# Lightning attention and top-1 routing on one core: half of an early first layer in Strassen's form, and the loads and lists around it

## The chip, the cores and the metric

The kernel runs on one NeuronCore of a Trainium2 chip. The metric is the device time of one execution in microseconds (us). PE (TensorE) does the matmuls, DVE (VectorE), ACT (ScalarE) and POOL (GpSimd) the elementwise work; SP (SyncE) only issues DMAs here. POOL also issues the indirect DMAs that gather rows by a list of indices, scatter rows, and store places into lists; ACT issues the stores of attention rows.

## The reference

Causal attention with a decay per head (4 batches, 8 heads, 768 positions, head width 64, all float32), then a top-1 mixture of experts over the 3072 rows of 512 that it gives:

```python
intra = einsum(qb, kb) * Dmask @ vb            # per block of 64, plus a carried state
inter = (qb * lam_pow) @ kv_state
x = attn_out.transpose(0, 2, 1, 3).reshape(3072, 512)
expert = argmax(x @ w_gate); gate = softmax(x @ w_gate)[expert]
for e in range(8):
    h  = maximum(x[mask_e] @ w1[e], 0)         # 512 -> 1024
    out[mask_e] = gate * (h @ w2[e])           # 1024 -> 512
```

## The kernel before, in words

**Attention.** The kernel goes through 12 steps: six chunks of 128 positions, each for two pairs of batches. A step transposes q and k, forms scores, applies the decay on DVE, and writes its finished rows to `xs` in DRAM. The gate's logits of each step are turned into a place on the chosen expert's list; POOL stores those places into `slots` in DRAM (L467), some of them behind a memset of `between` that fixes their position in POOL's stream.

**Passes.** A pass is a list of tokens of one expert: gathered rows `xg`, their transpose `xgT`, the first layer `hT` (8 chunks `fc` of 128 hidden features, contracted over 4 chunks `dc` of 128), the second layer, and a scatter of the rows. Expert 5's first 256 places are a pass of their own, 0a, which starts while the last attention step is still running. Pass 0b holds the rest of expert 5 (128 places). Passes 1 to 7 are the other experts, fullest first, with up to 418 places. 0a and 0b share one pair of weight tiles.

**Strassen's form.** Where a product of 2x2 blocks can be made with 7 block products in place of 8, the kernel does so (Winograd's variant): four sums of the left side, s1 to s4, four of the right side, t1 to t4, and sums u2, u3, u4 of the products. Before the change that holds for 0a's second layer (`form_early`, sums of `w2t` in `second_sums` and of `hT` in `left_of`, all on DVE), for the one tile of 0b's second layer (`lone_tile`, two products at a time on half of PE's rows each), and for both layers of passes 1 to 7 (`hidden_fast`, `outputs_across`). The first layers of 0a and 0b (`hidden`, L606) are plain products.

**What sets the order.** Each engine runs one stream of instructions in order. The framework writes that order when the kernel is built, with a planner that may move instructions; `pin` (keep_in_program_order) fixes those it is given among each other. DMAs of SP go out in the order of SP's stream. In program order, around the change: the last attention steps; `gather_early` (L1135 on), which issues the two gathers of 0a and then, when they have landed, the load of `w2t` (L1141); `turn(passes[0])`; the last stores of places; the counting that orders the experts (L1219 to L1254); the read of 0b's list, the value load that tells SP which expert is second, the read of pass 1's list (L496), the load of pass 1's `w1t` as one DMA of 2 MB (L202), and the gathers of 0b (one) and of pass 1 (four) (L527); then the loop over the passes. For pass 0a the loop makes `second_sums` on DVE (L683), `hidden`, `split(passes[2])` (copies of pass 1's rows into 16-bit planes on ACT, L575, and eight DMA transposes on SP, L577), SP's reads of the later lists, and `outputs_early`, which calls `turn(passes[1])` (0b's transposes on PE, L592) before its last product. For pass 0b it makes `hidden`, `first_sums` of pass 1's `w1t` on POOL (s3 and s1 at once, s2 and s4 in `finish`, L652 and L655), the gathers of pass 2, the sums of `later_sums`, `join` (two copies on ACT that put pass 1's `xgT` together, L585), `token_sums` on DVE (L713), and `lone_tile` (L782 and the sums after it, L818 to L835). `finish` waits for `token_sums`. The tile `xgT` has one buffer for all passes.

`form_early` ends with:

```python
        give(0, 1, product(a.s4, b.b22), u4)
        ahead()
        give(1, 0, product(a.a22, b.t4), u3)
```

Of the kernel before, what the change touches and what calls it, by code (L numbers as in the profile page):

```python
# [22 lines left out]
def kernel(  # L23
# [562 lines left out]

    def turn(m, pin=lambda inst: inst):
        m.xgT = ffn.tile([P, DC, m.n], F32, tag="xgT", name="xgT", bufs=1)
        for c in range(0, DC, 2):
            tp = bank(next(tp_banks), [P, 2, m.n], "tp")  # L590
            for dc, (t, w) in itertools.product(range(c, c + 2), enumerate(m.widths)):
                pin(nc.tensor.transpose(tp[:, dc - c, t * P:t * P + w],  # L592
                                        m.xg[t // 2][:w, t % 2, dc * P:(dc + 1) * P],
                                        ident[:w, :w]))

            if c == 0:
                nc.vector.tensor_copy(m.xgT[:, c:c + 2, :], tp)
            else:
                nc.scalar.copy(m.xgT[:, c:c + 2, :], tp)
# [12 lines left out]
    DH, FH = DC // 2, F // 2  # L612

    def form(product, sums_of, temps, give, first=nothing):

# [10 lines left out]
        give(0, 1, product(a.s4, b.b22), u2)  # L626
        give(1, 0, product(a.a22, b.t4), u3)

    def form_early(product, sums_of, temps, give, ahead):

        a, b = sums_of
        p1, u2, u3, u4 = temps
        nc.vector.tensor_copy(p1, product(a.a11, b.b11))
        give(0, 0, product(a.a12, b.b21), p1)
        nc.vector.tensor_add(u2, product(a.s2, b.t2), p1)
        nc.vector.tensor_add(u3, product(a.s3, b.t3), u2)
        p5 = product(a.s1, b.t1)
        give(1, 1, p5, u3)
        nc.vector.tensor_add(u4, p5, u2)
        give(0, 1, product(a.s4, b.b22), u4)  # L640
        ahead()
        give(1, 0, product(a.a22, b.t4), u3)
# [39 lines left out]
    def vector_sub(o, x, y):  # L682
        pin(nc.vector.tensor_sub(o, x, y))  # L683
# [107 lines left out]

    def outputs_early(m, w2, ahead):
        a = left_of(m.hT, 0, P, pair_rooms_of_sums())
        for make in (a.s3_made, a.s1_made, a.s2_made, a.s4_made):
            make()
        o, outs, temps = pair_rooms()

# [5 lines left out]

        form_early(block, (a, w2), temps, give, ahead)
        for i in range(2):
            scatter(at(m, i)[1], o[i])

# [327 lines left out]
    def gather_early(other):  # L1135
# [119 lines left out]


    def next_pass(i):
        e = nc.values_load(turns[0:1, i:i + 1], min_val=0, max_val=E - 1,
                           engines=[mybir.EngineType.SP])
        passes.append(make_pass(e, 0, CAPS[i], str(i)))  # L1260

    passes.append(make_pass(FIRST, EARLY, CAPS[0] - EARLY, "0b"))
    next_pass(1)
    later = []
    weights.append(load_weights(passes[2].w, later))
    for m in passes[1:]:
        fetch(m)
    last = E
    for i in range(last + 1):
# [16 lines left out]
        if i == 0:  # L1286
            w2 = second_sums(w2t, vector_sub)
        if i < 2:
            hidden(m, w1t)
# [78 lines left out]
```

## Time and profile before

| | us |
|---|---|
| median of 3 runs | 433.4 (432.65 to 434.5) |
| the profiled execution | 435.07 |
| its span, first to last instruction | 432.8 |
| PE busy | 421.3 (97%) |
| DVE, POOL, ACT busy | 266.0, 257.5, 176.8 |

The span is 2.3 us shorter than the profiled execution's time; that rest lies around the first and the last instruction. The profile gives for each instruction its start, its duration, and what ended its engine's idle time before it. A float32 matmul stands in the records as two (pass 0a's 32 matmuls of the first layer are 64 records). Records of pipelined matmuls overlap, so the pace of PE is read from the distance of their starts and not from the duration of one. The granted TensorE clock over the run is 0.997 of full speed, which is the level of 2.4 GHz nearly throughout.

### The profile page before, as it was taken

The numbers are of one execution on the slowest core, as the hardware profiler recorded it, in microseconds if no ns is written. First come the engines' busy times: TensorE is split into PE (matmuls) and PEld (weight loads), VectorE is DVE, ScalarE is ACT, GpSimd is POOL, SyncE is SP. The second block draws the span as 40 slices with busy tenths as digits, with TensorE's granted clock in tenths as the row PEclk, the third lists the DMA queues.
The fourth block names the chain that finished last, engine by engine and source line by source line (L and its number), as shares of the span: only waits on it lengthen the run. The fifth ranks groups of instructions, "written<-read, shape, count | busy, mean of one in ns | idle before, by whom it ended". The sixth has DMA issues, their size and how long they took to land.

```text
span 432.8 us, 9573 instructions
## 1 busy us (share of the span) xinstructions
PE 421.3 (97%) x3699; PEld 393.9 (91%) x3699; DVE 266.0 (61%) x585; ACT 176.8 (41%) x319; POOL 257.5 (59%) x205
## 2 busy tenths in 40 slices
PE   8999999999999999999999999999999999999993
PEld 6888898888888897999999999999999999999972
DVE  6656656566766647686547757755575664775463
ACT  3366545555542423450554155245424605422221
POOL 5243457373344368777948757693885887749032
PEclk9999999999999999999999999999999999999998
DMA  9999989999985758976369857965975894753122
GB/s 174 211 245 229 220 213 213 233 193 249 292 283 149 265 105 234 325 246 237 52 139 190 332 76 157 319 179 112 299 246 81 196 384 80 153 186 56 20 83 63
DMA packets 164727, 83.49 MB, mean 193 GB/s; under 512 B 146019, under 2 KB 146063, under 8 KB 164672
## 3 DMA queue, kind: packets, MB, share of 16 engines
q1 hardware_dynamic: 155024, 63.21, 61.2%
q0 software_dynamic: 5712, 13.26, 10.2%
q10 hardware_dynamic: 3936, 6.31, 4.2%
q8 instruction: 31, 0.51, 0.5%
q14 instruction: 24, 0.20, 0.2%
HBM read 58.96 MB, written 13.09 MB: 166 GB/s over the span
## 4 chain that ended last, share of the span: by engine, by line
PE 87%; DMA 4%; issue 3%; ACT 2%; POOL 1%; SPq 1%; DVE 1%; POOLq 0%; ACTq 0%
PE p L728 30%; PE p L914 26%; PE sp L279 5%; PE ph L606 5%; PE op L314 4%; PE p L774 3%; DMA v_in<-in_v_dram 3%; PE cp L340 2%; PE tx L376 2%; PE tk L241 2%; PE tq L241 2%; PE op L305 2%; PE p L782 2%; PE lgT L366 1%; DMA xg<-xs,list_0a 1%
## 5 line engine op out<-in xcount | busy, mean ns | idle before, releaser
L533 POOL DMA_INDIRECT out_dram<-o_room,list x24 | 25.7, 1069 | 51.9 <-DMA decay<-planes_q 22.4
L286 DVE TENSOR_TENSOR mt<-sp,decay 128x512 f32<-128x512 f32 x48 | 30.1, 684 | 23.8 <-PE sp L279 18.6
L739 ACT ACTIVATE hT<-hT 128x418 f32<-128x418 f32 (+6 forms) x56 | 28.3, 521 | 34.1 <-DVE hT L736 31.2
L728 PE MATMUL p<-xgT,w1t 128*128 128x209 f32 (+6 forms) x224 | 41.4, 327 | 0.0
L728 PEld LDWEIGHTS p<-xgT,w1t 128*128 128x128 f32 x224 | 37.1, 189 | 0.8 <-issue 0.8
L618 ACT COPY u_qT<-p 128x418 f32<-128x418 f32 (+6 forms) x14 | 6.7, 479 | 69.5 <-PE p L728 69.5
L914 PE MATMUL p<-hT,w2t 128*128 128x209 f32 (+5 forms) x192 | 33.6, 328 | 0.0
L914 PEld LDWEIGHTS p<-hT,w2t 128*128 128x128 f32 x192 | 32.0, 189 | 0.0
L467 POOL DMA_INDIRECT slots<-entry,slot_i x24 | 23.8, 990 | 13.1 <-PE tl L391 5.9
L527 POOL DMA_INDIRECT xg<-xs,list x25 | 25.9, 1034 | 9.0 <-issue 6.1
L736 DVE TENSOR_TENSOR hT<-p,u_kd 128x418 f32<-128x418 f32 (+6 forms) x28 | 15.6, 559 | 21.0 <-PE p L728 21.0
L279 PE MATMUL sp<-qT,kT 64*128 64x128 f32 x384 | 27.5, 293 | 0.4 <-ACT kT L263 0.4
L279 PEld LDWEIGHTS sp<-qT,kT 64*128 64x128 f32 x384 | 24.3, 199 | 3.0 <-issue 2.0
L269 POOL TENSOR_TENSOR kd<-k_in,kdec 128x512 f32<-128x512 f32 x12 | 12.4, 1042 | 23.7 <-PE cp L340 11.9
L655 POOL TENSOR_TENSOR s_q<-w1t 128x1024 f32<-128x1024 f32 x7 | 16.5, 2363 | 16.6 <-DVE t_xT L713 14.6
L326 ACT COPY xT<-op 128x512 f32<-128x512 f32 x12 | 7.0, 585 | 36.9 <-PE op L314 33.8
L606 PE MATMUL ph<-xgT,w1t 128*128 128x256 f32 (+1 forms) x128 | 21.6, 328 | 0.0
L606 PEld LDWEIGHTS ph<-xgT,w1t 128*128 128x128 f32 x128 | 19.2, 191 | 1.7
L728 PE MATMUL p<-t_sd,w1t 128*128 128x209 f32 (+6 forms) x112 | 20.7, 327 | 0.0
L728 PE MATMUL p<-st,s_q 128*128 128x209 f32 (+6 forms) x112 | 20.7, 327 | 0.0
L652 POOL TENSOR_TENSOR w1t<-w1t 128x1024 f32<-128x1024 f32 x7 | 20.2, 2892 | 0.6
L728 PE MATMUL p<-t_xT,w1t 128*128 128x209 f32 (+6 forms) x112 | 20.6, 326 | 0.0
(252 smaller groups left out, 1093.9 us busy)
## 6 DMA issues: line engine op xcount, KB each, us to landing
w2t<-in_moe_w_dram SPq DMA_DIRECT2D x8, 2048.0 KB
w1t<-in_moe_w_dram SPq DMA_DIRECT2D x7, 2048.0 KB
xs<-x_room ACTq DMA_DIRECT2D x12, 512.0 KB
v_in<-in_v_dram SPq DMA_DIRECT2D x8, 512.0 KB
o_room<-qs_room SPq DMA_DIRECT2D x76, 48.0 KB
q_in<-in_q_dram SPq DMA_DIRECT2D x7, 512.0 KB
k_in<-in_k_dram SPq DMA_DIRECT2D x7, 512.0 KB
room<-in_q_dram SPq DMA_DIRECT2D x4, 512.0 KB
```

Of the source, the lines that this page charges most:

```text
L241: pin(nc.tensor.transpose(t[:, i, b, :], src[:, b, h:h + 2, :], ident))
L279: m.scored = pin(nc.tensor.matmul(sp[u][:, i, b, :], lhsT=m.kT[s][halves[u], i, b, :], rhs=m.qT[s][halves[u], i, b, :], start=(i == 0 and ...
L286: nc.vector.tensor_mul(mt[:, u], sp[u], decay[:, u, s * HP // 2:(s + 1) * HP // 2].unsqueeze(2).to_broadcast(shp))
L314: pin(nc.tensor.matmul(out_at(m, b, u, hp), lhsT=m.v[:, b, 2 * hp + u, :], rhs=m.mt[hp // 2][:, u, hp % 2, b, :], start=(first and hp == 0 ...
L467: put = nc.gpsimd.indirect_dma_start(out=slots, out_offset=bass.IndirectOffsetOnAxis(ap=slot_i[:, i:i + 1], axis=0), in_=entry[:, n, bs[i] ...
L527: return nc.gpsimd.indirect_dma_start(out=dst, out_offset=None, in_=xs[:rows, :], in_offset=bass.IndirectOffsetOnAxis(ap=idx, axis=0))
L533: put = nc.gpsimd.indirect_dma_start(out=out, out_offset=bass.IndirectOffsetOnAxis(ap=idx, axis=0), in_=src, in_offset=None, bounds_check= ...
L606: nc.tensor.matmul(ph, lhsT=w1t[:, dc, fc * P:(fc + 1) * P], rhs=m.xgT[:, dc, :], start=(dc == 0), stop=(dc == DC - 1))
L652: return nc.gpsimd.tensor_tensor(out=o, in0=x, in1=y, op=ALU.add)
L728: nc.tensor.matmul(p[:, i, :], lhsT=lhs[:, dc, g, i * P:(i + 1) * P], rhs=rhs[:, dc, :], start=(dc == 0), stop=(dc == DH - 1))
L739: pin(nc.scalar.activation(outs[i][k], outs[i][k], ACT.Relu))
L914: nc.tensor.matmul(p[:, c, :], lhsT=lhs[:, f, c * P:(c + 1) * P], rhs=rhs[:, f, :], start=(f == 0), stop=(f == FC // 2 - 1))
```

## The change

1. **0a's first layer.** Its first four chunks of hidden features stay plain products. The last four are made in Strassen's form (`hidden_early`): seven products of 128 token columns, each 4 matmuls. The sums of `w1t` (`early_sums`, four of 128x512) run on POOL, put in its stream behind 0a's gathers and ahead of the last stores of places. The sums of `xgT` (128x256 each), and the adds u2, u3, u4 and of `hT`, run on DVE; ACT copies p1 and applies the relu. DVE's four sums of `w2t` are put between those adds (`others`).
2. **0a's second layer.** `outputs_early` has its seven products in another order, with fixed banks, and its sums of `hT` in the order s1, s2, s3, s4. The scatter of the second tile is called before 0b's transposes, which now come ahead of the product s4 x b22.
3. **Loads and lists.** SP first loads the number of the second expert, then issues the first half of its `w1t` (1 MB), then reads pass 1's list, then 0b's, then issues the second half. Pass 1's gathers come before 0b's.
4. **Room.** 0b's `xgT` lies in a part of `qs_room` and not in the tile `xgT`.

```diff
-    def turn(m, pin=lambda inst: inst):
-        m.xgT = ffn.tile([P, DC, m.n], F32, tag="xgT", name="xgT", bufs=1)
+    def turn(m, pin=lambda inst: inst, room=None):
+        m.xgT = room
+        if room is None:
+            m.xgT = ffn.tile([P, DC, m.n], F32, tag="xgT", name="xgT", bufs=1)
...
+    def early_sums(w1t):
+        w = w1t.rearrange("p (j d) (g i f) -> p i j d g f", j=2, g=2, i=2)
+        a = [[w[:, i, j, :, 1] for j in range(2)] for i in range(2)]
...
+        pin(pool_sub(s3, a[0][0], a[1][0]))
+        pin(pool_add(s1, a[1][0], a[1][1]))
+        pin(pool_sub(s2, s1, a[0][0]))
+        pin(pool_sub(s4, a[0][1], s2))
...
+    def hidden_early(m, w1t, a, others):
+        h = m.n // 2
+        m.hT = ffn.tile([P, FC, m.n], F32, tag="hT", name="hT", bufs=1)
+        for fc in range(FC // 2):
+            ph = bank(next(ph_banks), [P, m.n], "ph")
+            for dc in range(DC):
+                nc.tensor.matmul(ph, lhsT=w1t[:, dc, fc * P:(fc + 1) * P], rhs=m.xgT[:, dc, :],
+                                 start=(dc == 0), stop=(dc == DC - 1))
+            relu(1, m.hT[:, fc, :], ph)
...
+        b = right_sums(b, t1, t2, t3, t4, vector_sub)
...
+        x1 = product(a.a11, b.b11, 0)
+        pin(nc.scalar.copy(p1, x1))
+        x7 = product(a.s2, b.t2, 1)
+        ready(0, 0, product(a.a12, b.b21, 0, x1))
+        others.pop(0)()
+        add(u2, x7, p1)
+        x3 = product(a.s3, b.t3, 2)
+        others.pop(0)()
+        add(u3, x3, u2)
+        x6 = product(a.a22, b.t4, 3)
+        others.pop(0)()
+        add(outs[1][0], x6, u3)
+        ready(1, 0)
+        x5 = product(a.s1, b.t1, 6)
+        add(outs[1][1], x5, u3)
+        ready(1, 1)
+        add(u4, x5, u2)
+        others.pop(0)()
+        add(outs[0][1], product(a.s4, b.b22, 1), u4)
+        ready(0, 1)
...
-        for make in (a.s3_made, a.s1_made, a.s2_made, a.s4_made):
-            make()
...
-        form_early(block, (a, w2), temps, give, ahead)
-        for i in range(2):
-            scatter(at(m, i)[1], o[i])
+        a.s1_made()
+        a.s2_made()
+        pin(nc.vector.tensor_copy(p1, block(a.a11, b.b11, 7)))
+        a.s3_made()
+        a.s4_made()
+        give(0, 0, block(a.a12, b.b21, 4), p1)
+        p6 = block(a.a22, b.t4, 5)
+        add(u2, block(a.s2, b.t2, 7), p1)
+        add(u3, block(a.s3, b.t3, 4), u2)
+        give(1, 0, p6, u3)
+        p5 = block(a.s1, b.t1, 7)
+        give(1, 1, p5, u3)
+        add(u4, p5, u2)
+        scatter(at(m, 1)[1], o[1])
+        ahead()
+        give(0, 1, block(a.s4, b.b22, 4), u4)
+        scatter(at(m, 0)[1], o[0])
...
         hold(begun[0], other)
+        m.sums = early_sums(weights[0][0])
         behind = nc.sync.dma_start(out=w2t, in_=w2_r[FIRST])
...
-    passes.append(make_pass(FIRST, EARLY, CAPS[0] - EARLY, "0b"))
-    next_pass(1)
-    later = []
-    weights.append(load_weights(passes[2].w, later))
-    for m in passes[1:]:
-        fetch(m)
+    e = next_expert(1)
...
+    parts = [lambda p=p: pin(nc.sync.dma_start(out=w1t[:, p], in_=pick(w1_r, e)[:, p]))
+             for p in (slice(0, DC // 2), slice(DC // 2, DC))]
+    parts[0]()
+    late = [make_pass(e, 0, CAPS[1], "1", pin),
+            make_pass(FIRST, EARLY, CAPS[0] - EARLY, "0b", pin)]
+    parts[1]()
+    passes += late[::-1]
+    short_room = qs_room[:, 2].rearrange("p i b c -> p (i b) c")
...
+    for m in late:
+        fetch(m, pin=pin)
...
-            w2 = second_sums(w2t, vector_sub)
-        if i < 2:
+            others = []
+            w2 = second_sums(w2t, lambda *x: others.append(lambda: vector_sub(*x)))
+            hidden_early(m, w1t, m.sums, others)
+        elif i < 2:
             hidden(m, w1t)
...
-            outputs_early(m, w2, lambda: turn(passes[1], pin))
+            outputs_early(m, w2, lambda: turn(passes[1], pin, short_room))
```

## Rows read from the trace of the kernel before

**Rows 1.** The page's first part: busy time of each engine.

```profile
PE 421.3 (97%) x3699; PEld 393.9 (91%) x3699; DVE 266.0 (61%) x585; ACT 176.8 (41%) x319; POOL 257.5 (59%) x205
```

**Rows 2.** The chain that ended last, in order of time, from the end of attention to pass 1: start, length (us), what, and the number of records.

```profile
119.02 3.63 DMA xg<-xs,list_0a
...
127.81 12.19 PE ph L606 x56
140.00 10.36 PE p L774 x48
150.36 0.44 PE tp L592 x4
...
152.53 7.14 PE ph L606 x64
159.67 6.11 PE p L782 x48
...
166.33 0.35 issue
...
167.76 19.96 PE p L728 x110
```

**Rows 3.** Busy time in stretches of 0a's and 0b's first layers: length, then busy us and count of PE, PEld, DVE, ACT, POOL, then the granted clock, the DMA engines' share and GB/s.

```profile
125.50:140.00 14.50, 14.44 (x71) 12.35 (x70) 9.87 (x41) 3.50 (x12) 8.00 (x12) 1.00 0.63 204
152.50:159.70 7.20, 7.20 (x66) 7.08 (x65) 2.52 (x8) 0.00 (x0) 5.74 (x3) 1.00 0.60 141
```

**Rows 4.** DVE in order of time: start, length, line, operation, in brackets the idle time before it and what ended it.

```profile
130.06 0.19 DVE L1246 TENSOR_SCALAR turns<-of_r 128x7 int32<-128x7 f32 x1
133.90 1.23 DVE L683 TENSOR_TENSOR t_q<-w2t 128x1024 f32<-128x1024 f32 x1 [2.77 <-DMA w2t<-in_moe_w_dram]
...
141.18 0.69 DVE L754 TENSOR_TENSOR h_kT<-h_qT,hT 128x512 f32<-128x512 f32 x1
142.97 0.56 DVE L800 TENSOR_SCALAR o_room<-x_room,list_0a 128x256 f32<-128x256 f32 x1
143.65 0.49 DVE L801 SCALAR_TENSOR_TENSOR o_room<-p,list_0a,o_room 128x256 f32<-128x256 f32 x1
149.07 0.41 DVE L639 TENSOR_TENSOR x_room<-p,x_room 128x256 f32<-128x256 f32 x1
160.70 0.42 DVE L754 TENSOR_TENSOR qs_room<-qs_room,hT 128x256 f32<-128x256 f32 x1
166.19 0.43 DVE L819 TENSOR_TENSOR u_t<-p,u_t 64x256 f32<-64x256 f32 x1
```

**Rows 5.** ACT in order of time, columns as in rows 4.

```profile
140.04 0.38 ACT L559 ACTIVATE hT<-ph 128x256 f32<-128x256 f32 x1 [1.34 <-PE ph L606]
146.70 2.18 ACT L575 COPY planes_q<-xg 128x512 uint16<-128x512 uint16 x4 [6.28 <-DMA xg<-xs,list]
159.75 2.09 ACT L585 COPY xgT<-decay 128x1672 uint16<-128x1672 uint16 x1 [8.31 <-PE ph L606]
161.70 2.07 ACT L585 COPY xgT<-across 128x1672 uint16<-128x1672 uint16 x1
```

**Rows 6.** POOL in order of time, columns as in rows 4.

```profile
88.14 1.04 POOL L352 TENSOR_TENSOR sd<-st,sdec 128x512 f32<-128x512 f32 x1
102.35 0.96 POOL L467 DMA_INDIRECT slots<-entry,slot_i  x1 [0.19 <-issue]
108.99 0.77 POOL L496 DMA_DIRECT2D list_0a<-slots  x1 [5.68 <-DMA slots<-entry,slot_i]
125.96 1.00 POOL L467 DMA_INDIRECT slots<-entry,slot_i  x1 [5.85 <-PE tl L391]
132.33 0.96 POOL L467 DMA_INDIRECT slots<-entry,slot_i  x1 [0.30 <-issue]
137.96 1.54 POOL L527 DMA_INDIRECT xg<-xs,list_0b  x1 [4.67 <-DMA list_0b<-slots]
139.81 0.97 POOL L527 DMA_INDIRECT xg<-xs,list  x1 [0.30 <-issue]
143.72 0.88 POOL L527 DMA_INDIRECT xg<-xs,list  x1 [0.31 <-issue]
166.41 2.38 POOL L655 TENSOR_TENSOR s_q<-w1t 128x1024 f32<-128x1024 f32 x1
191.65 3.04 POOL L652 TENSOR_TENSOR w1t<-w1t 128x1024 f32<-128x1024 f32 x1
```

**Rows 7.** The DMA queue of SP (q1) in the stretch 119 to 120 us: packets, MB, share of the 16 engines.

```profile
q1 hardware_dynamic: 10, 0.02, 4.3%
```

**Rows 8.** SP's issues in order of time.

```profile
135.15 0.34 SPq L496 DMA_DIRECT2D list_0b<-slots  x1
136.83 0.38 SPq L202 DMA_DIRECT2D w1t<-in_moe_w_dram  x1
147.35 1.32 SPq L577 DMA_TRANSPOSE decay<-planes_q  x1
156.80 1.19 SPq L577 DMA_TRANSPOSE across<-planes_k  x1
```

**Rows 9.** Stretches of 1 us, columns as in rows 3.

```profile
134.00:135.00 1.00, 1.00 (x6) 0.89 (x5) 1.00 (x1) 0.38 (x2) 0.00 (x0) 1.00 0.00 0
...
145.00:146.00 1.00, 1.00 (x6) 0.88 (x5) 0.42 (x1) 0.00 (x0) 0.00 (x0) 1.00 1.06 410
```

More of the change, by code (lines that the diff above doesn't have):

```diff
@@ L612 @@
     DH, FH = DC // 2, F // 2
+    def early_sums(w1t):
+        w = w1t.rearrange("p (j d) (g i f) -> p i j d g f", j=2, g=2, i=2)
+        a = [[w[:, i, j, :, 1] for j in range(2)] for i in range(2)]
+        q, k = (qkv.tile([P, 2, DH, FH // 2], F32, tag=t, name=f"e_{t}") for t in "qk")
+        s1, s2, s3, s4 = q[:, 0], q[:, 1], k[:, 0], k[:, 1]
+        pin(pool_sub(s3, a[0][0], a[1][0]))
+        pin(pool_add(s1, a[1][0], a[1][1]))
+        pin(pool_sub(s2, s1, a[0][0]))
+        pin(pool_sub(s4, a[0][1], s2))
+        return SimpleNamespace(a11=a[0][0], a12=a[0][1], a22=a[1][1], s1=s1, s2=s2, s3=s3, s4=s4)
@@ new lines, in hidden_early, with product, add, ready @@
+    def hidden_early(m, w1t, a, others):
[7 more added lines that the diff above has]
+            relu(1, m.hT[:, fc, :], ph)
+        b = [[m.xgT[:, j * DH:(j + 1) * DH, k * h:(k + 1) * h] for k in range(2)] for j in range(2)]
+        t1, t3, t4 = (work.tile([P, DH, h], F32, tag=t, name=f"e_{t}", bufs=n)
+                      for t, n in (("sd", 2), ("sd", 2), ("xT", 1)))
+        t2 = st.rearrange("p b g d -> p (b g d)")[:, :DH * h].rearrange("p (c n) -> p c n", c=DH)
+        b = right_sums(b, t1, t2, t3, t4, vector_sub)
+        p1, u2, u3 = thirds(h)
+        u4 = work.tile([P, 2, h], F32, tag="kT", name="u_4")
+        c = FC // 2
+        outs = [[m.hT[:, c + 2 * i:c + 2 * i + 2, k * h:(k + 1) * h] for k in range(2)]
+                for i in range(2)]
+        def product(lhs, rhs, at, onto=None):
+            p = bank(at, [P, 2, h], "pe") if onto is None else onto
+            for i in range(2):
+                for dc in range(DH):
+                    pin(nc.tensor.matmul(p[:, i, :], lhsT=lhs[:, dc, i * P:(i + 1) * P],
+                                         rhs=rhs[:, dc, :], start=(onto is None and i == dc == 0),
+                                         stop=(i == 1 and dc == DH - 1),
+                                         skip_group_check=True))
+            return p
+        def add(*x):
+            pin(nc.vector.tensor_add(*x))
+        def ready(i, k, src=None):
+            pin(nc.scalar.activation(outs[i][k], outs[i][k] if src is None else src, ACT.Relu))
+        x1 = product(a.a11, b.b11, 0)
[18 more added lines that the diff above has]
+        ready(0, 1)
@@ L626, in form @@
         give(0, 1, product(a.s4, b.b22), u2)
[L627 to L641, printed above, removed]
         give(1, 0, product(a.a22, b.t4), u3)
@@ L790, in pair_rooms, with outputs_early @@
         return o, outs, [u[:, i, :] for i in range(4)]
-    def outputs_early(m, w2, ahead):
+    def outputs_early(m, b, ahead):
         a = left_of(m.hT, 0, P, pair_rooms_of_sums())
-        for make in (a.s3_made, a.s1_made, a.s2_made, a.s4_made):
-            make()
-        o, outs, temps = pair_rooms()
+        o, outs, (p1, u2, u3, u4) = pair_rooms()
+        add = nc.vector.tensor_add
         def give(i, k, p, u):
```

11 lines of the change are left out of this document (8 added, 3 removed).

## The prediction

> **What bounds the kernel now.** I read the page's busy shares first: PE is busy 97% of the span and no other engine more than 61% [rows 1]. Then the chain of waits, from the end of attention on. From 127.8 us it is PE and nothing else: 0a's first layer, its second layer with 0b's four transposes in it, 0b's first layer, its second layer, pass 1, with one hole of 0.35 us at 166.33 [rows 2]. So between 125.5 and the end a change can win only what it takes off PE's stream, and that hole. It can lose more: DVE, POOL, ACT and the DMAs have slack here, and the question is whether the change uses it up. The DMA engines are at rest at 134 us and full at 145 us [rows 9].
>
> **PE's work in 0a's first layer.** 56 records of 256 columns take 12.19 us, so one takes 0.2177 us; 0b's 64 records of 128 columns take 7.14 us, so one takes 0.1116 us [rows 2]. The half that changes is 4 chunks x 4 matmuls x 2 records = 32 records of 256 columns, 6.97 us. In its place stand 7 products x 4 matmuls x 2 records = 56 records of 128 columns, 6.25 us. Saved: 0.72 us. The shape is that of 0b's first layer, whose weight loads are already busy for 7.08 of 7.20 us [rows 3], so 0.1116 is taken as it is. The second layer keeps its 56 records (48 in 10.36 us) and its 0.44 us of transposes [rows 2]: 0.
>
> **DVE's work for it.** DVE is idle from 131.1 to 133.9, until `w2t` lands [rows 4]. Four sums of 128x256 at 0.42 us (the 160.70 row) are 1.7 us and fit there. If they were put earlier they would push the ordering of the experts, which ends at 130.25 [rows 4]; that number is needed first for the load of item 3, which stands behind `w2t` in SP's queue until about 133, so up to some 2 us cost nothing.
>
> From 133.9 DVE has the four `w2t` sums (1.23 each) and six adds of 128x256 (0.41 to 0.45, taken as 0.45 with the gap): 4.9 + 2.7 = 7.6 us, so the last part of `hT` is written at 141.5 and its relu (0.38, rows 5) is done at 141.9. PE by then: plain half 125.5 + 6.97 + 0.6 of short products between (14.50 less 64 x 0.2177, rows 3) = 133.1, seven products to 139.3, then a11 x b11 to 141.1 and a12 x b21 to 142.8 (8 records x 0.216 = 1.73 each, from 10.36/48). The third, a22 x t4, is the first that needs the relu at 141.9: slack 0.9 us. s1 and s2 (0.69 and a gap of 0.04 each) end at 143.4, wanted at 144.5: slack 1.1. s3, s4 and the scaling of the first tile (0.56 + 0.49) end at 146.0, when bank 4 is wanted again at 146.2: slack 0.2. The price of all this is between 0 and 1.5 us (six adds, 2.7, less the 1.2 us that DVE now idles before its second sum of `hT`). I take 0, since each step has its slack, though the last is thin.
>
> **POOL's sums ahead of the last stores.** No such sum of two 128x512 blocks is in the trace. The nearest rows are a 128x512 product at 1.04 us and a 128x1024 sum at 2.38 us, half of it 1.19; the slowest, beside DVE's adds, took 3.04, half 1.52 [rows 6]. Four take 4.2 to 6.1 us; I take 4.8. The place for them is POOL's idle 5.85 us before the store at 125.96 [rows 6], and their input is there: SP's queue moves its last 10 packets of `w1t` after 119 us, 0.02 MB [rows 7]. So they end at 124.9 and the stores don't move; at the far bound they move by 0.3 us. Behind them wait the six stores up to 132.33, and all list reads.
>
> Here a rule of the Trainium skill speaks against the change: its page "GPSIMD Engine Reference", section "8. Key points", says that GpSimd shares its SBUF interfaces with VectorE and contends with DVE instructions that have two SBUF inputs. DVE has only short instructions in that stretch, and the 3.04 against 2.38 us is what the trace shows of it; by the rule the sums end up to 0.3 us late, by the rows alone they are on time.
>
> **Loads and lists.** SP waits for the order of the experts (130.25) and then for the last store (issued at 132.33 to 133.29) before it reads 0b's list at 135.15; `w1t` goes out only at 136.83 [rows 4, 6, 8]. The DMA engines rest meanwhile and are then at 410 GB/s while the gathers and 2 MB of `w1t` compete [rows 9]: pass 1's first gather, issued at 139.81, lands only at 146.70 [rows 5, 6], 6.9 us, where 0a's took 3.63 [rows 2]. After the change 1 MB goes out at about 131.5. At the 410 GB/s of the full stretch it takes 2.6 us; it shares SP's queue with `w2t`, which DVE has by 133.9, so it moves from about 133 to 136 and fills the rest. Pass 1's list is read first; its first gather starts at 137.96 + d, where d is the delay that the load ahead gives the last stores and the list reads, with 0 <= d <= 3.8 (the last store of before had landed 1.86 us after its issue ended at 133.29; one of the busy attention steps, ended at 103.31, took 5.68 [rows 6, 8]). I take d = 1: the load is over by 136. The first gather then starts at 139.0 instead of 139.81 with half the traffic beside it, and the transposes start 1 to 3 us before 147.35 [rows 8]. 0b's gather is now the fifth: its issue starts at 143.7 + d and it lands 3.63 to 6.9 us after, 148.3 to 151.6, and PE turns it after six products, at 139.3 + 6 x 1.73 = 149.7. With most of `w1t` moved by then I take the lower end: no wait, but a bound of 1.9 us.
>
> **Room and the hole.** ACT's join waited 8.31 us and began at 159.75, when PE's last record of 0b's first layer freed `xgT` [rows 2, 5]. With 0b's rows elsewhere it waits for the transposes alone, whose last was issued at 156.80 [rows 8]. With those 1 to 3 us earlier, join (until 163.77, rows 5) and DVE's token sums end earlier, DVE's first add of `lone_tile` is no longer as late as 166.19 [rows 4], and the last pair of products, which needs the bank that it reads, follows without the hole: 0.35 us. s_q then starts before 166.41 [rows 6], as PE wants it.
>
> **Sum.** -0.72 - 0.35 = -1.07 us; everything after 167.76 is PE's stream [rows 2] and moves with it. 435.07 - 1.07 = 434.0 for an execution like the profiled one. That one lies 1.7 above the median of 433.4; from the median, 432.3.
>
> **Rivals.**
> *DVE becomes the bound in 0a.* For: 7.6 us of DVE work in a row behind `w2t`, slack of 0.2 to 1.1 us, and a program order in which an add waits for a sum of a tile that has just landed. Against: each slack is positive. If `w2t` lands 1 us later or the adds are put worse, PE loses 0.7 to 1.5 us: 433.0 to 433.8, about 433.4.
> *The join does not move.* For: eight transposes at 1.2 to 1.3 us each are a chain of SP, whatever the loads do. Against: it started when pass 1's first rows landed. If so, PE comes 0.72 us early to work that starts no sooner, the hole grows to 1.07, and the time stays: 433.4.
> *Late lists (the slower side).* The load ahead of the lists delays the stores and reads. From d = 2.4 on 0b's rows land, even at 3.63 us, after PE wants them (143.7 + 2.4 + 3.6 = 149.7); PE's stream is in order, so all behind waits. At d = 3.8 they land at 151.1 to 154.4, a stall of 1.4 to 4.7 us, middle 3: 433.4 - 0.7 + 3.0 = 435.7. For: the 5.68 us row; against: it is from steps with q, k and v in small packets, and the 1 MB is over 3 us after it begins. The Trainium skill ("DMA: Bandwidth & Descriptors", "Queues, rings and completion order") says that each DMA engine takes turns between queues at whole packets; by that d is above 0. The run of before has no such load there.
> *It does more.* Only if work outside PE's stream was shortened, for which no row speaks.
>
> **Numbers.** Forecast 0.60 (its own range 431.5 to 433.2); DVE 0.12; join 0.10; late lists 0.11; anything else, such as another order by the planner, 0.07. From these, 430.9 to 435.3 holds the time 8 times in 10, late lists partly included; the low end leaves 1.4 us for the spread that the three runs of before show (432.65 to 434.5). 0.5% is 2.2 us, about what can be told from no change. The forecast is half of that: faster 0.12 (forecast plus a lucky spread), slower 0.12 (late lists and 0.01), same 0.76.
>
> **What would show it.** Right: 56 records at 0.11 us in 0a's products without gaps; POOL's sums between 120 and 125 and the store still at 126; `w1t` packets between 133 and 136; join before 158; no hole near 166. Wrong: PE waiting for DVE before a22 x t4 or s3 x t3; PE waiting for 0b's rows at its transposes; the list reads after 137; or a gap that opens in pass 1 or later, where no row says one is near.

## The result, and the profile after

The changed kernel is slower: median 437.5 us against 434.0 us of the kernel before on the same chip (22 runs each), ratio 1.0056 (95% interval 1.0034 to 1.0079). The forecast was 432.3 and the range ended at 435.3. The first profiled execution of the changed kernel (442.1 us) was a disturbed one, so the rows of after come from a second profile of the same kernel (437.8 us, span 436.0), taken in this run:

> The changed kernel as it is, looked at again. Late-lists theory: the last stores land 5 to 8 us after their issue beside the first half of the second expert's w1, the list reads fall at 138 to 141 us, and PE waits 1 to 3.5 us at the transposes of 0b's rows on the gather by the list of 0b. The rest of the loss (the 3.4 us of the first profile's slower clock behind that wait) is gone if the clock does not fall there. Rival (the lists cost nothing and the loss is the clock alone): no wait above 0.5 us at 0b's transposes, the lists read before 137 us.

Its ratio was 1.0086 (1.0050 to 1.0122). The page's first part, which answers to [rows 1]:

```profile
PE 419.2 (96%) x3723; PEld 392.8 (90%) x3723; DVE 270.1 (62%) x595; ACT 177.3 (41%) x320; POOL 262.4 (60%) x209
```

PE does 2.1 us less work and the span is 3.2 us longer: PE waits. Where it waits stands in the view of waits on PE, from 113 us to pass 1 (releaser, total, count, longest):

```profile
PE tp L594 <- DMA xg<-xs,list_0b: 2.8, 1, 2.8
PE rank L441 <- DVE oh L417: 0.5, 1, 0.5
PE pe L653 <- ACT u_qT L666: 0.4, 1, 0.4
PE rank L441 <- DVE slot_i L465: 0.2, 1, 0.2
```

PE in order of time, columns as in rows 4; compare [rows 2]:

```profile
131.54 1.05 PE L653 MATMUL pe<-xgT,w1t 128*128 128x128 f32 x8
132.43 1.06 PE L653 MATMUL pe<-st,e_q 128*128 128x128 f32 x8
133.88 1.16 PE L653 MATMUL pe<-xgT,w1t 128*128 128x128 f32 x8 [0.39 <-ACT u_qT L666]
134.87 1.06 PE L653 MATMUL pe<-e_sd,e_k 128*128 128x128 f32 x8
...
138.45 3.62 PE L831 MATMUL p<-w2t,hT 128*128 128x256 f32 x16
...
151.73 0.63 PE L594 MATMUL tp<-ident,xg 128*128 128x128 f32 x4 [2.76 <-DMA xg<-xs,list_0b]
152.19 3.29 PE L831 MATMUL p<-w2t,h_kd 128*128 128x256 f32 x8
155.28 7.63 PE L608 MATMUL ph<-qs_room,w1t 128*128 128x128 f32 x64
```

The starts show three things. A product of 8 records takes 0.89 us, as forecast, but the third starts 1.45 us after the second: it adds onto the first product (`onto` x1, a12 x b21 onto a11 x b11) in the same bank, and must wait until that one is copied out. The transposes of 0b's rows wait 2.76 us. And behind that wait the next product takes 3.09 us from start to start, where one takes 1.73 us: the granted clock (third number from the end) had fallen from 1.00 towards the level of 1.2 GHz after PE had waited for 2.8 of the 4 us from 148 to 152:

```profile
148.00:150.00 2.00, 0.97 (x5) 1.00 1.00 110
150.00:152.00 2.00, 0.27 (x3) 1.00 1.12 293
152.00:154.00 2.00, 2.00 (x10) 0.63 0.86 211
154.00:156.00 2.00, 2.00 (x8) 0.52 0.42 85
156.00:158.00 2.00, 2.00 (x20) 1.00 0.25 61
```

Why the rows are late stands in the chain of waits and in SP's and POOL's rows, beside [rows 6, 8]. First the chain (start, length, what):

```profile
130.77 5.83 DMA slots<-entry,slot_i
...
137.21 3.18 DMA list<-slots
...
147.00 4.59 DMA xg<-xs,list_0b
```

Then SP's issues:

```profile
130.72 0.01 SPq L1340 DMA_DIRECT2D w1t<-in_moe_w_dram  x1
137.21 0.38 SPq L496 DMA_DIRECT2D list<-slots  x1
...
138.60 1.12 SPq L1340 DMA_DIRECT2D w1t<-in_moe_w_dram  x1
```

The last store is issued 0.05 us after the first half of `w1t`, and lands 5.83 us later; before, 0b's list was read 2.82 us after the last store's issue. The first list read is at 137.2 us, a little earlier than the 138 to 141 expected for this run, and the clock fell again. The traffic of 131 to 134 us (packets, MB, share) shows who had the engines:

```profile
q1 hardware_dynamic: 100, 0.41, 73.1%
q0 software_dynamic: 13, 0.00, 0.3%
```

q1 carries the load, q0 the store. The load starts slowly. These are its packets in 131 to 132 and in 134 to 135 us:

```profile
q1 hardware_dynamic: 10, 0.04, 81.8%
q1 hardware_dynamic: 101, 0.41, 100.4%
```

In the first stretch 10 packets take 81.8% of the 16 engines' time, 1.3 us each; in the second one takes 0.16 us. From 131 to 133 us 30 packets of the load move and none of the store, though POOL has done with the store's issue at 131.82. The store's packets come 13, 19, 28 and 4 in the four us from 133 on, beside the load at full pace; 34 of the stores before it had moved in 130 to 131 us. The load of before, issued at 136.83 behind the stores, starts in the same way (33 GB/s in 137 to 138 us, 90 in the next, 410 in the third).

From here on a table helps. It cuts PE's stream of each profile by the starts of four records: **A** from the last step's scores x values (L314, 32 records) to 0a's first record; **B** from there to 0a's second layer; **C** from there to 0b's four transposes; **D** from there to pass 1's second layer. After that PE's stream takes 236.39 us from pass 1's second layer to its last block of products, before and after, so the change acts on A to D alone. What comes earlier differs from profile to profile (that first record starts between 116.8 and 119.6 us), and so does the rest behind the last block (8.2 to 9.9 us), so one profile's span says less than these stretches.

| us | A | B | C | D | sum |
|---|---|---|---|---|---|
| before | 6.36 | 14.33 | 10.36 | 37.36 | 68.41 |
| changed | 6.93 | 14.50 | 13.28 | 38.00 | 72.71 |
| forecast for the change | 6.36 | 13.61 | 10.36 | 37.01 | 67.34 |
| loads alone | 7.92 | 14.33 | 11.97 | 37.71 | 71.93 |
| changed, lists first | 8.07 | 14.37 | 10.36 | 37.02 | 69.82 |
| changed, 0b's list first | 6.92 | 14.50 | 10.36 | 38.82 | 70.60 |
| changed, half behind the stores | 7.14 | 14.55 | 12.26 | 36.32 | 70.27 |
| Strassen alone | 6.92 | 14.32 | 10.36 | 37.55 | 69.15 |
| same, no GpSimd sums | 6.55 | 14.34 | 10.36 | 37.57 | 68.82 |
| Strassen, early list | 6.92 | 14.52 | 10.37 | 37.05 | 68.86 |
| same, no sums | 6.76 | 14.40 | 10.37 | 37.63 | 69.16 |
| Strassen, early list, copy on DVE | 6.92 | 14.26 | 10.36 | 37.50 | 69.04 |
| same, no sums | 6.54 | 14.23 | 10.36 | 36.65 | 67.78 |
| before, early list | 6.31 | 14.33 | 10.36 | 37.36 | 68.36 |
| before, room | 6.39 | 14.32 | 10.36 | 36.95 | 68.02 |
| before, both | 6.49 | 14.32 | 10.36 | 36.30 | 67.47 |

A holds, in some profiles, a wait for 0a's rows (1.6 us in lists first, 1.4 in loads alone, 0.6 in half behind the stores, at most 0.3 in the others). Those rows hang on stores and a list read of about 100 to 110 us, ahead of all that the change touches; the wait is left out of what follows.

### The profile page after: what moved, and what is told of

It is laid out like the page before. It is cut to its first block, busy times and chain, and to the rows that moved or that the text cites. A ratio compares the mean times of both kernels' runs of the same rounds, so it can differ in the third digit from the quotient of the medians.

```text
span 440.3 us, 9649 instructions
## 1 busy us (share of the span) xinstructions
PE 423.8 (96%) x3723; PEld 397.5 (90%) x3723; DVE 266.1 (60%) x595; ACT 177.5 (40%) x320; POOL 262.6 (60%) x209
## 3 DMA queue, kind: packets, MB, share of 16 engines
q10 hardware_dynamic: 3936, 6.31, 4.3%
## 4 chain that ended last, share of the span: by engine, by line
PE 84%; DMA 5%; issue 3%; POOL 2%; ACT 2%; DVE 1%; SPq 1%; POOLq 0%; ACTq 0%
PE p L785 29%; PE p L984 25%; PE sp L279 6%; PE op L314 4%; PE tx L376 3%; PE cp L340 3%; PE tk L241 2%; PE op L305 2%; PE tq L241 2%; PE ph L608 2%; PE lgT L366 2%; PE p L839 2%; DMA slots<-entry,slot_i 1%; DMA xg<-xs,list_0b 1%; PE p L831 1%
## 5 line engine op out<-in xcount | busy, mean ns | idle before, releaser
L527 POOL DMA_INDIRECT xg<-xs,list x25 | 27.6, 1103 | 15.1 <-DMA list<-slots 8.7
L785 PE MATMUL p<-xgT,s_v 128*128 128x209 f32 (+6 forms) x112 | 20.5, 326 | 0.0
L785 PE MATMUL p<-xgT,s_k 128*128 128x209 f32 (+6 forms) x112 | 20.5, 326 | 0.0
L1027 ACT ACTIVATE o_room<-o_room,list 128x512 f32<-128x512 f32 (+6 forms) x22 | 14.1, 709 | 14.8 <-DMA o_room<-qs_room 14.8
```

Of the source, the lines that this page charges most:

```text
L527: return nc.gpsimd.indirect_dma_start(out=dst, out_offset=None, in_=xs[:rows, :], in_offset=bass.IndirectOffsetOnAxis(ap=idx, axis=0))
L785: nc.tensor.matmul(p[:, i, :], lhsT=lhs[:, dc, g, i * P:(i + 1) * P], rhs=rhs[:, dc, :], start=(dc == 0), stop=(dc == DH - 1))
```

## The experiments

**The loads and lists.** Loads alone is the kernel before with the change's item 3:

```diff
...
+    parts[0]()
+    late = [make_pass(e, 0, CAPS[1], "1", pin),
+            make_pass(FIRST, EARLY, CAPS[0] - EARLY, "0b", pin)]
+    parts[1]()
...
```

> The kernel before with only the loads, list reads and gathers of the change (half of w1t ahead of the lists, pass 1 before 0b). Load theory and order theory: PE waits 3 to 5 us for 0b's rows at its transposes and then runs at the lower clock for some us, ratio 1.005 to 1.012. Strassen theory: ratio 0.999 to 1.001.

Measured: ratio 1.0057 (1.0026 to 1.0088). SP, and the chain:

```profile
132.77 0.70 SPq L1269 DMA_DIRECT2D w1t<-in_moe_w_dram  x1
140.73 0.38 SPq L496 DMA_DIRECT2D list<-slots  x1
```

```profile
132.78 7.33 DMA slots<-entry,slot_i
...
143.52 4.35 DMA xg<-xs,list
```

PE waits 1.4 us for 0b's rows, where 3 to 5 was expected, and the granted clock stays at 1.00 behind that wait. In time these loads alone cost what the whole change costs; in this profile C and D are 1.96 us longer than before. Lists first is the changed kernel with both halves behind the list reads:

```diff
-    parts[0]()
     late = [make_pass(e, 0, CAPS[1], "1", pin),
             make_pass(FIRST, EARLY, CAPS[0] - EARLY, "0b", pin)]
+    parts[0]()
     parts[1]()
```

> The changed kernel with both halves of the second expert's w1t issued behind the two list reads; nothing else. Load theory (the half ahead holds up the last stores of places, and through them the lists and 0b's rows): SP reads the lists at 135 to 137.5 us and not at 140.5, PE waits under 0.5 us at 0b's transposes, ratio to the kernel before 0.996 to 0.999. Order theory (0b's gather being the fifth is enough): PE still waits 2 us or more there, ratio 1.002 or more. Strassen theory (the sums on VectorE and GpSimd cost the time): no change against the changed kernel, ratio about 1.006.

Measured: 1.0016 (0.9991 to 1.0042). The lists are read at 136.08 and 136.53 and no wait is left at 0b's transposes (C is 10.36). Most of the loss is gone, but nothing is gained (0.996 to 0.999 was expected). The next two look for another order. The first keeps the early half and reads 0b's list, and gathers its rows, first:

```diff
-    late = [make_pass(e, 0, CAPS[1], "1", pin),
-            make_pass(FIRST, EARLY, CAPS[0] - EARLY, "0b", pin)]
+    late = [make_pass(FIRST, EARLY, CAPS[0] - EARLY, "0b", pin),
+            make_pass(e, 0, CAPS[1], "1", pin)]
...
```

> The changed kernel with the half of w1t still ahead, but 0b's list read and 0b's gather first again. Load theory: the lists are still read at about 140 us; 0b's rows land at 148 to 151, PE waits 0 to 1 us for them; pass 1's rows come about 1.5 us later than in the changed kernel, so a wait of 0 to 2 us may open at pass 1's first products; ratio 0.998 to 1.004. Order theory: as with the lists of before, no wait at all, ratio 0.996 to 0.999. Strassen theory: about 1.006.

Measured: 1.0067 (1.0035 to 1.0100), above what was expected. C is whole again, but pass 1's rows are now late: D is 38.82, with 1.2 us on POOL's s_q and 0.7 us on ACT's copy of 0b's rows. The second lets POOL issue the half, on its own queue, behind the last store:

```diff
-    store_places(len(waiting), lambda inst: inst)
+    store_places(len(waiting), pin)
...
-    parts[0]()
+    e_pool = nc.values_load(turns[0:1, 1:2], min_val=0, max_val=E - 1,
+                            engines=[mybir.EngineType.Pool])
+    pin(nc.gpsimd.dma_start(out=w1t[:, :DC // 2], in_=pick(w1_r, e_pool)[:, :DC // 2]))
```

> The changed kernel with the first half of the second expert's w1t issued by GpSimd behind the last store of places, on GpSimd's own DMA queue, and not by SP ahead of the list reads. Load theory (a big load that is under way holds back the stores' packets in the other queue): the stores are ahead of it now, so SP reads the lists at 135 to 137.5 us and not at 138 to 140.5; PE waits 0 to 1 us for 0b's rows; ratio 1.000 to 1.003, like the run with the lists ahead of w1t. If any load at that time delays the lists: list reads at 138 or later and ratio 1.005 or more.

Measured: 1.0031 (0.9998 to 1.0063). The store lands 2.63 us after its issue, but the list read at 135.21 now takes 5.36 us, and 0b's rows are 1.7 us late. The load holds up whatever small transfer comes beside it, stores or list.

**Strassen's form alone.** The changed kernel with the loads, lists and gathers of before:

> The changed kernel with the loads, list reads and gathers of the kernel before (0b's list first, one load of 2 MB behind both lists); Strassen's form, the new order of the second layer and 0b's room stay. Load theory and order theory: PE has no wait at 0b's transposes, 0a's seven products take 6.25 us, ratio 0.996 to 0.999 (0.72 us off PE's stream and 0.35 us of the hole). Strassen theory: ratio 1.004 or more, with a gap on PE in 0a's products or behind late stores.

Measured: 1.0040 (1.0016 to 1.0063), so this half of the change loses too. DVE's short operations, in order of time:

```profile
120.03 3.00 DVE L465 CAST slot_i<-slot 128x2 int32<-128x2 f32 x1
123.03 0.23 DVE L393 TENSOR_REDUCE lg<-tl 128x16 f32<-128x64 f32 x1
...
123.49 0.88 DVE L402 TENSOR_TENSOR sh<-lg,mx 128x16 f32<-128x16 f32 x1
124.30 0.68 DVE L599 COPY xgT<-tp 128x512 f32<-128x512 f32 x1
124.90 0.83 DVE L407 SCALAR_TENSOR_TENSOR key<-sh,rev 128x16 f32<-128x16 f32 x1
```

Beside them POOL makes its sums:

```profile
121.70 1.29 POOL L709 TENSOR_TENSOR e_q<-w1t 128x512 f32<-128x512 f32 x1
123.07 1.27 POOL L712 TENSOR_TENSOR e_q<-e_q,w1t 128x512 f32<-128x512 f32 x1
124.42 1.28 POOL L712 TENSOR_TENSOR e_k<-w1t,e_q 128x512 f32<-128x512 f32 x1
```

The cast ends at 123.03, L402 at 124.37 and L407 at 125.73; the three sums beside them end at 122.99, 124.34 and 125.70. DVE's long operations end where a sum of POOL ends: what they lose is the rest of the sum that is under way.

The next run leaves these sums out. Its products read `w1t`'s blocks in their place, so half of 0a's hidden features come from wrong left sides:

```diff
...
-        pin(pool_sub(s3, a[0][0], a[1][0]))
...
-        pin(pool_sub(s4, a[0][1], s2))
+        s1, s2, s3, s4 = a[1][0], a[1][1], a[0][0], a[0][1]
```

> The kernel of the run with Strassen's form alone, without the four sums of w1t on GpSimd: the products read blocks of w1t in their place, so half of 0a's hidden features are computed from the wrong left sides; products, adds and all else stay. Port theory (those sums hold up VectorE's short instructions, and through them PE's first rank products): VectorE's instructions between 118 and 128 us take 0.16 to 0.25 us each again (they took up to 3.0), PE no longer waits 0.2 to 0.4 us for them, and the time falls by 0.5 to 0.9 us against the run with the sums: ratio to the kernel before 1.000 to 1.002. If the sums cost nothing there: ratio stays at 1.003 to 1.005. In both PE still waits about 1 us or more for s_q in pass 1's second product, since 0a's products end 0.7 us early and s_q does not.

Measured: 0.9994 (0.9972 to 1.0015), and the same operations of DVE:

```profile
118.77 0.43 DVE L465 CAST slot_i<-slot 128x2 int32<-128x2 f32 x1
121.77 0.23 DVE L393 TENSOR_REDUCE lg<-tl 128x16 f32<-128x64 f32 x1 [2.57 <-PE tl L391]
...
122.23 0.17 DVE L402 TENSOR_TENSOR sh<-lg,mx 128x16 f32<-128x16 f32 x1
122.67 0.69 DVE L599 COPY xgT<-tp 128x512 f32<-128x512 f32 x1 [0.27 <-PE tp L594]
123.28 0.16 DVE L407 SCALAR_TENSOR_TENSOR key<-sh,rev 128x16 f32<-128x16 f32 x1
```

The cast lost nothing: in both kernels DVE goes on 3.00 us after it began, when PE's `tl` is there. L402 (0.88 for 0.17) and L407 (0.83 for 0.16) stand on the path to the ranks: 1.4 us. The reductions and the copy between them lost nothing. That fits the Trainium skill's "GPSIMD Engine Reference", section "8. Key points": the contention is with DVE instructions that have two SBUF inputs, and those two have them. The cast has one; the page also names DVE modes that use two ports, and no run here shows whether the cast is in one.

Without the sums A is 0.37 us shorter (6.55 for 6.92) and 0a's plain half takes 7.41 us in place of 7.61; B does not shrink (14.34 for 14.32), since PE then waits longer at the third product. In time the three pairs of runs with and without the sums do not agree: 1.0040 and 0.9994 here, 0.9982 and 1.0008, 0.9986 and 0.9993 further down. Only the stretches show a price.

**Where the 0.72 us go.** Strassen alone, with the sums and without them, still waits 1.0 us in D for POOL's s_q (s2 of pass 1), which stands on POOL behind pass 2's gathers. One try put s_q and s_v ahead of those gathers, which for pass 0b are then called behind `finish`:

```diff
-        if 0 < i < last - 1:
+        if 1 < i < last - 1:
             fetch(passes[i + 2], pin=pin)
...
+            fetch(passes[i + 2], pin=pin)
```

> The kernel of the run with Strassen's form alone, with pass 1's last two sums on GpSimd (s_q, s_v) ahead of the four gathers of pass 2. Chain theory (PE's gain is lost because s_q comes behind gathers that hang on the list reads behind the transposes): s_q starts at the end of the token sums, about 2 us earlier, PE's wait of 0.98 us before pass 1's second product goes, ratio 0.002 to 0.003 below that of the run with Strassen's form alone. If the join or the transposes are the limit instead: s_q starts less than 0.5 us earlier and the ratio stays. If pass 2's later rows matter: a new wait at pass 2's first products, ratio above.

Measured: 1.0174 (1.0123 to 1.0224). s_q came at 163.54 and its wait was gone, but the gathers came only at 170.25 to 174.95, and ACT, whose stream holds the copies of those rows ahead of pass 1's relus, made PE wait 4.6 us until 184.39 and the clock fall: behind D this run is 8.2 us longer than the others. The same edit without the sums on POOL measured 1.0158 (1.0113 to 1.0202), where 0.9965 to 0.9990 was expected; PE waits 4.7 us at the same place. The other end of the chain is better. In Strassen alone the gathers wait for their list:

```profile
162.91 0.99 POOL L527 DMA_INDIRECT xg<-xs,list  x1 [2.74 <-DMA list<-slots]
...
167.84 2.37 POOL L712 TENSOR_TENSOR s_q<-w1t 128x1024 f32<-128x1024 f32 x1
```

SP reads that list at 160.18, behind the eight transposes. The next runs read it right behind pass 1's list:

```diff
     next_pass(1)
+    next_pass(2)
...
-                for j in range(2, E):
+                for j in range(3, E):
```

> Strassen alone with the loads of before, and SP reads pass 2's list right behind pass 1's, ahead of the transposes of pass 1's rows (where it was read behind them, at 160.2 us). Chain theory (the 0.72 us are swallowed because POOL's s_q stands behind pass 2's gathers, and those behind a late list read): the list is read before 145 us, the gathers start at 158 to 161 us instead of 162.9, s_q starts at about 165.5 instead of 167.84, and the wait of 0.98 us on s_q ahead of pass 1's second product goes to below 0.2. The waits of PE on VectorE's rank work beside the GpSimd sums (0.6 to 0.8 us in all) stay, so the time comes to 0.9 to 1.0 us less than Strassen alone: ratio 0.999 to 1.002. Rival (the join limits pass 1 whatever the list does): the gathers start earlier but s_q does not, since the token sums on POOL stand ahead of it and end at about 165.7; the wait stays near 1.0 us and the ratio near 1.004.

Measured: 0.9982 (0.9956 to 1.0008). The gathers start at 158.07, s_q at 164.72, and PE waits for it no more. It waits instead 0.45 us ahead of the last pair of 0b's second layer, for DVE's first add, the hole of before, though 0b's rows have their own room:

```profile
158.07 0.99 POOL L527 DMA_INDIRECT xg<-xs,list  x1
...
164.72 2.36 POOL L712 TENSOR_TENSOR s_q<-w1t 128x1024 f32<-128x1024 f32 x1 [1.93 <-DVE t_xT L770]
```

```profile
165.09 1.08 PE L839 MATMUL p<-w2t,qs_room 128*64 128x256 f32 x8 [0.45 <-DVE u_t L889]
```

s_q itself now waits for DVE's token sums, which stand behind the join. The same without the sums on POOL (the products read `w1t`'s blocks again):

> As the run before it, but the four GpSimd sums of w1t blocks are left out and the products that read them read w1t's blocks instead, so half of the early tokens' hidden features come from wrong left sides; the work on PE and VectorE is unchanged. With both hindrances away (VectorE's short instructions held up by GpSimd's sums, s_q behind a late list) the 0.72 us of PE must show at the end: ratio 0.996 to 0.999, no wait ahead of pass 1's second product above 0.3 us. Rival (a third limit, the join through GpSimd's token sums): ratio 0.999 to 1.001, with a new wait between 0b's last product and pass 1's second one.

Measured: 1.0008 (0.9976 to 1.0040), a miss, and the rival of a third limit came true:

```profile
166.54 1.08 PE L834 MATMUL p<-w2t,qs_room 128*64 128x256 f32 x8 [0.62 <-DVE u_t L884]
```

D is 37.63, and B is 14.40 where 13.61 was due. Both hindrances were away and PE's saving was still not there, so my account was incomplete in two places. In D it is the join that comes late, since pass 1's rows do: ACT's first copy of them starts 29.8 us after the start of A with Strassen's form and the early list, 30.0 here, and 27.2 in the kernel before with the same list and room (at the end of this section). There SP reads the first list 2.4 us after the last store's issue, here 4.1 to 4.3 us; why stays open. And 0.79 us goes already in B, at the third product. Its wait is for ACT's copy, and ACT stands so in the changed kernel:

```profile
128.29 0.38 ACT L559 ACTIVATE hT<-ph 128x256 f32<-128x256 f32 x1 [1.45 <-PE ph L635]
132.90 0.66 ACT L559 ACTIVATE hT<-ph 128x256 f32<-128x256 f32 x2 [4.23 <-PE pe L653]
133.44 0.38 ACT L666 COPY u_qT<-pe 128x256 f32<-128x256 f32 x1
```

The third relu of the plain half was due 1.73 us after the second and came 4.61 us after it. Two runs let DVE make the copy, the second again without the sums:

```diff
-        pin(nc.scalar.copy(p1, x1))
+        pin(nc.vector.tensor_copy(p1, x1))
```

> As the run with Strassen and the early list, but VectorE copies the first product a11 x b11 out of its bank, which ScalarE did behind two relus of the plain half that came 1.5 to 3 us late. Theory (ScalarE's late relus hold that copy, and TensorE's third product, which adds into the same bank, waits for it): the wait of 0.4 us and the gap of 0.6 to 0.7 us at the third product go, the 56 products take 6.2 to 6.4 us instead of 6.9, and the ratio falls by 0.0012 to 0.0017, to about 0.997. Rival (what is late is TensorE's own signal for that product, whoever copies): the gap stays at 0.5 us or more with VectorE as the engine waited for, and the ratio stays at 0.998. Second rival (VectorE becomes the bound, its sums of w2t starting 0.5 us later): waits of TensorE for VectorE's adds between 134 and 144 us.

> The same without the four GpSimd sums of w1t blocks (half of the early tokens' hidden features come from wrong left sides). With all three hindrances gone (VectorE's short work held up, the third product behind ScalarE, s_q behind a late list) the saving of 0.72 us must show on top of what the early list alone gave before's kernel (ratio 0.9958): ratio 0.993 to 0.996, and from the start of 0a's first product to its second layer 13.5 to 13.7 us where the kernel before took 14.3. Rival (something else still swallows it): ratio 0.997 or above with a wait of TensorE between 139 us and pass 1 that is larger than 0.3 us.

Measured: 0.9986 (0.9947 to 1.0024) and 0.9993 (0.9960 to 1.0027). In the first of them:

```profile
132.54 1.06 PE L653 MATMUL pe<-st,e_q 128*128 128x128 f32 x8
133.03 0.66 ACT L559 ACTIVATE hT<-ph 128x256 f32<-128x256 f32 x2 [4.25 <-PE pe L653]
133.26 0.42 DVE L666 COPY u_qT<-pe 128x256 f32<-128x256 f32 x1 [1.70 <-PE pe L653]
...
133.74 1.16 PE L653 MATMUL pe<-xgT,w1t 128*128 128x128 f32 x8
```

The gap shrinks from 0.56 to 0.31 us, but the 56 records still take 6.66 us (6.2 to 6.4 expected) and the ratio does not fall: D is 37.50, with 0.4 us of wait for DVE's first add again. DVE is idle and still sees the first product only at 133.26, 0.7 us after PE's records of it give way to the next. So the rival holds in part: the signal of PE is late, whoever copies. In the second run B is 14.23, against 13.5 to 13.7 expected, and the ratio misses what was expected too.

**What helped.** The kernel before with the early list (the edit above) and the change's room for 0b's rows, and each alone:

```diff
...
+    short_room = qs_room[:, 2].rearrange("p i b c -> p (i b) c")
...
-            outputs_early(m, w2, lambda: turn(passes[1], pin))
+            outputs_early(m, w2, lambda: turn(passes[1], pin, short_room))
```

> The kernel before without Strassen, with the change's separate room for the transposed rows of pass 1 and pass 2's list read early. Chain theory: the wait on s_q of before is only some 0.35 us, so at most that comes off: 0.2 to 0.4 us, ratio 0.998 to 1.000. Rival (the earlier gathers of pass 2 take DMA time from what pass 1 waits for): ratio above 1.001 with a new PE wait on a DMA.

> The kernel before with pass 2's list read early and nothing else; 0b's transposed rows stay in pass 1's room, so the join still waits for 0b's first layer. List theory (the gain of before with both came from s_q no longer standing behind a late list): ratio 0.995 to 0.998, s_q ahead of TensorE's need. Room theory (the gain came from the join that starts earlier): ratio 0.999 to 1.001 and the gap of 0.35 us ahead of the last pair of 0b's second layer still there.

> The kernel before with the change's separate room for 0b's transposed rows and nothing else. Room theory: the join starts with the last transpose, at 158 instead of 159.75, the gap of 0.35 us at 166.33 goes, ratio 0.996 to 0.999. List theory: the join is earlier, but POOL's gathers still wait for the list read behind the transposes, s_q starts no earlier than 166, and the ratio is 0.999 to 1.001.

Measured: both 0.9958 (0.9932 to 0.9984), median 432.96 against 434.76; list alone 0.9990 (0.9957 to 1.0022); room alone 0.9968 (0.9936 to 0.9999). In D the list alone gives nothing, since the gap ahead of the last pair is still there:

```profile
164.75 1.08 PE L784 MATMUL p<-w2t,qs_room 128*64 128x256 f32 x8 [0.34 <-DVE u_t L821]
```

The room alone gives 0.41 and then meets a new wait:

```profile
170.32 1.69 PE L730 MATMUL p<-t_sd,w1t 128*128 128x209 f32 x8 [0.39 <-ACT u_qT L620]
```

Both give 1.06, more than expected, with no wait in D. The interval of both lies below before; that of room alone does so barely (to 0.9999), and no other's does. That both lie below room alone is not shown by the times, whose intervals overlap; it rests on D.

## Why the prediction was wrong

**0a's first layer, -0.72 in B: +0.17.** The pace held (0.111 us a record), and the step "in its place stand 7 products x 4 matmuls x 2 records ... 6.25 us" failed in taking the sum of the records for the length of the stretch. They take 6.91 us (131.54 to 138.45): the wait of the third product on the copy of the first takes 0.56 us, the restart behind it 0.10. The other 0.24 is PE's wait for the rank work, behind POOL's sums. I had worked out the slack of every sum and add, and not this wait, though it was in the diff. Even with a punctual signal the slack is small: from the end of the first product PE has 0.89 us of other work, of which ACT's usual delay behind PE (some 0.2), the copy (0.38) and PE's start behind it (0.06, from 133.44 + 0.38 to 133.88) fill 0.64.

**DVE's work.** The four sums of `xgT` and the adds cost PE nothing that the waits show before pass 1; the slacks worked out for a22 x t4 and later held. The DVE rival named a loss of this kind and size (0.7 to 1.5) on the wrong engine and two products too late.

**POOL's sums.** Place and length were right: 117.86 to 123.1 us in a profile that lies 2.1 us earlier, 1.27 to 1.30 each for 1.2. The effect was taken the wrong way round: "by the rule the sums end up to 0.3 us late". They were hardly slower; DVE's two-input operations were five times as long, each until a sum ended, and DVE stood on the path to PE's ranks. A is 0.57 longer in this profile and PE waits 0.24 in B, against 0 in the sum. Runs without the sums give back 0.16 to 0.38 in A and at most 0.12 in B, and the times show no price that all pairs share.

**Loads and lists.** The step that decided the sign: "I take d = 1: the load is over by 136". Pass 1's first gather started at 141.34, in a profile 2.1 us early, so d was 141.34 + 2.13 - 137.96 = 5.5 us, above the bound of 3.8 as well. Of it 0.57 is A, 3.6 the store (137.21 - 130.77 for 135.15 - 132.33) and 1.3 the list read (141.34 - 137.21 for 137.96 - 135.15). The bound held one store against the row of 5.68; here the last store (5.83) and behind it the list read (3.18) were both slow, one after the other. And the load was not over after 2.6 us at 410 GB/s: with its slow start it took from 130.7 to 136 us, which is 132.9 to 138 in the forecast's time. 0b's gather, now the fifth, landed 2.76 us late. The rival "late lists" had mechanism, place and sign, 435.7 us, and a chance of 0.11. Its price left out the clock: the records behind the wait ran at the lower level for some 4 us, 1.7 us in D.

The rule weighed there, turns between queues at whole packets ("DMA: Bandwidth & Descriptors", "Queues, rings and completion order" in the Trainium skill), has the right sign. But the trace shows 100 packets of the load against 13 of the store from 131 to 134 us, and none of the store in the first two of these, so equal turns do not give the size of d. Whether the profile's packets are those that the page counts is not shown here.

**Room and the hole, -0.35: held where pass 1's rows are in time.** Room alone takes the gap away (D -0.41). In the changed kernel D without the clock's 1.7 us is 36.30, as in the kernel before with room and early list, 1.06 below before; there PE's wait in C had given the join 2.8 us. The forecast gave no condition for it: it needs s_q early as well, and in Strassen alone, where the list is read late, s_q takes it back (D 37.55). With Strassen's form and the early list the hole itself is back, since the join is late.

**"The join does not move"** was half a rival: what did not move in Strassen alone was not the join, but pass 2's list and gathers ahead of s_q. With the list early it was the join: D is 37.05 to 37.63 there (36.65 in the last run without the sums), where 36.30 was to be had.

Together: +0.57 in A, +0.17 in B, +2.92 in C, +0.64 in D, 4.30 us in this profile, where -1.07 was forecast. The times say 2.4 to 3.7 us (0.0056 and 0.0086 of 434).

## What to carry to other kernels

Before a large load is put ahead of small transfers, ask which instruction reads what the small ones write: two or three small DMAs in a chain (store, list, gather) can each pay for the load beside them, and the wait at the end can cost the clock as well. Before a saving on the busiest engine is counted, look for every product that adds onto a bank that another engine must first read; the length of a stretch is the sum of its records only if no such wait is in it. And an engine off the path that gets new work can slow a neighbour that is on it: in the changed kernel PE waited 0.8 us for VectorE operations that 5.2 us of GpSimd sums had held up, and Strassen's form had 0.72 us to give.

## What the runs showed of the hardware

- Two-input sums of 128x512 on GpSimd (1.27 to 1.31 us each) lengthen DVE's 128x16 operations with two inputs from 0.17 to 0.83 and 0.88 us, and a cast of 128x2 from 0.43 to 3.00 us. In all nine profiles with these sums every such longer operation ends within 0.04 us of the end of a sum (in Strassen alone 124.37 and 124.34); where one met only the last 0.09 us of a sum (lists first, 121.76 to 121.93) it took 0.17. So it is held for the rest of the sum under way, and not slowed throughout. Reductions and a copy out of PSUM beside the same sums stay at 0.17 to 0.23 and 0.68 us.
- PE's signal to ACT and DVE comes late around 130 to 134 us in all profiles of this study but one, the kernel before included: the third relu follows the second after 2.69 to 4.66 us instead of 1.73. In the kernel before it is 3.42 (129.68, 133.10) and costs nothing; in the changed kernel it is 4.61. The one is the first profile of the changed kernel (442.1 us), where PE came 3.4 us later to that place: there it was 1.73 and the 56 records took 6.25 us without a gap. What delays it stays open: no run takes a single suspect away.
- A load of `w1t` starts slowly: in the changed kernel its packets of 4 KB take 1.3 us each in its first stretch (131 to 132 us) and 0.16 us each three us later, and the store issued beside it (130.77 to 131.82) moves its first packets after 133.
- After PE had been idle for 2.8 of 4 us the granted clock was 0.63 and 0.52 over the next 4 us and 1.00 after that; one product of 8 records took 3.09 us in place of 1.73.
